# Attention and maxout FFN in one kernel: transposed attention, column halves issued alternately, one attention step per FFN step

## The chip, the cores and the metric

One core of a Trainium2 chip. The metric is device time in microseconds (us), the median over executions of the same program. Ratios are computed as the mean time of one kernel's runs over that of the other's of the same rounds, so a ratio is not quite the quotient of the medians that are quoted; intervals are 95%.

## The reference

```python
# attention with projected keys and values; B=8 batches, H=8 heads, S=1024, D=64, 64 projected rows
k_proj = einsum('ks,bhsd->bhkd', E, k)
v_proj = einsum('ks,bhsd->bhkd', F, v)
scores = q @ k_proj^T / sqrt(D)
attn   = exp(scores - max) / sum
x      = attn @ v_proj            # then heads side by side: 8192 tokens x 512
# maxout FFN
h   = max(x @ w1, x @ w2, x @ w3) # 512 -> 768
out = h @ w_out                   # 768 -> 512
```

Neither kernel subtracts the maximum before the exponential.

## The kernel before

For each batch the attention is built first and the FFN of the previous batch after it; a scheduler interleaves the two on TensorE. The matmuls of both kernels write to PSUM, a memory that is used here in pieces of 128 x 512 fp32 values, called banks. Attention has five of them, the FFN three. These parts are changed:

```python
# k projection: both halves of the heads go to partitions 0..63
for hh in range(2):
    for si in range(SI):
        matmul(out=kp_ps[0:64, hh*256:(hh+1)*256], lhsT=eT[:, si, :], rhs=k_t[:, hs, si, :])
# v projection: even heads to partitions 0..63, then odd heads to 64..127
for par, vt in ((0, vp_e), (1, vp_o)):
    for si in range(SI):
        matmul(out=vt[rows, 0:256], lhsT=fT[:, si, :], rhs=v_t[:, par::2, si, :])
...   # kpT_bd and vp_bd (block diagonals of two heads) are zeroed again for every batch
# attention times v: tokens on partitions; a column of ones in vp_bd gives the softmax sum
for si in range(8):
    for u in range(2):
        for gg in range(2):
            matmul(out=av_v[:, gg, 0:130], lhsT=pT[g][:, si, :], rhs=vp_bd[:, g, :])
        reciprocal(zinv, sums)                       # DVE
        tensor_tensor(x_sb, av, zinv, mult)          # DVE
    for ct in range(4):
        transpose(out=xt_v[:, ct, 0:128], in_=x_flat[:, ct*128:(ct+1)*128])
    copy(xT[:, :, si, :], xt_v)                      # ACT
...
# FFN, the same in both kernels: 12 matmuls of 512 columns per step, then
copy(h1s, h_ps[0])                                   # ACT
max(m12, h_ps[1], h1s); max(hT, h_ps[2], m12)        # DVE
```

The softmax here doesn't subtract the row's maximum and nothing guards it: scores larger than these inputs give would overflow.

## Time and profile before

| | before |
|---|---|
| median of 6 runs | 467.17 us (466.78 to 468.32) |
| span of the profiled execution | 465.2 us |
| TensorE busy | 93% |
| one batch (first k projection matmul to the next batch's), called the pitch below | 52.88 us |
| of it FFN, 192 matmuls x 216 ns | 41.45 us |
| last matmul starts | 459.40 us |

The profile's lines for the busy shares, the chain, one batch and the windows stand in the prediction. One more view is needed, the 40 slices of the span: a digit is the busy share of a slice in tenths (9 is 90% or more), and PEclk is the granted TensorE clock. A slice is 11.6 us. After them stand three lines of the start, DVE's timeline and TensorE's; in brackets is an idle time and who ended it.

```profile
PE   1475999999999999999999999999999999999995
PEclk9999999999999999999999999999999999999999
...
40.84 0.43 DVE L135 COPY q_p<-q_t 128x1024 bf16<-128x1024 bf16 x1 [2.51 <-DMA q_t<-in_q_dram]
41.19 0.24 DVE L209 RECIPROCAL zinv<-ps_s 128x4 f32<-128x4 f32 x2
...
41.88 0.39 PE L220 MATMUL ps_s<-ident,x_sb 128*128 128x128 bf16 x2 [2.77 <-DVE x_sb L210]
```

TensorE is full from the fifth slice on and stays full to the end. Before that, DVE waits 2.51 us for the q of the second batch, with the first batch's reciprocals behind it in its queue, and TensorE waits for them in turn. A time can therefore fall in two ways only: fewer nanoseconds of TensorE per batch, times the 7 batches that lie beside an FFN, or an earlier start. To keep the two apart, this text uses the prediction's "effective start": the start of the last matmul, less 331.8 us of FFN matmuls, less 7 times what attention and its waits hold TensorE per batch (the pitch less 41.45). For the kernel before it is 459.40 - 331.8 - 7 x 11.43 = 47.6 us. (192 x 0.216 is 41.47; 41.45 is the prediction's figure and is used throughout, which moves every effective start by the same 0.1.)

### The profile page before, as it was taken

What the parts mean: (1) busy time and instruction counts of PE and PEld (TensorE: products, weight loads), DVE (VectorE), ACT (ScalarE), POOL (GpSimd) and SP (SyncE); (2) the same over time, 40 slices, a digit from 0 to 9 for tenths busy, and PEclk for the clock granted to TensorE, in tenths of its full rate; (3) what the DMA queues carried; (4) which work ended last, traced back from release to release, by engine and by line L of the source; (5) the groups of instructions that cost most, each with busy time, mean ns of one, the idle gap of its engine ahead of it and who ended that gap; (6) DMA issues with size and microseconds to landing.
All of it is one profiled execution on the core that took longest, in us unless ns stands there. A gap on an engine that the chain in (4) does not pass through costs nothing.

```text
span 465.2 us, 6667 instructions
## 1 busy us (share of the span) xinstructions
PE 432.2 (93%) x2623; PEld 227.3 (49%) x2672; DVE 229.1 (49%) x550; ACT 173.4 (37%) x311; POOL 54.7 (12%) x74
## 2 busy tenths in 40 slices
PE   1475999999999999999999999999999999999995
PEld 1344555455544555455544555455544555444442
DVE  2026575527934375426935376425935277334351
ACT  1142555235432543235532553235432453322322
POOL 7212240004000320005000320001000000000000
PEclk9999999999999999999999999999999999999999
DMA  7999999319620691209720591202020200202102
GB/s 112 206 211 205 208 205 207 118 80 173 111 92 0 144 201 20 92 42 192 129 92 1 134 197 32 92 0 92 2 91 0 92 1 0 92 0 92 56 36 90
DMA packets 30207, 45.78 MB, mean 98 GB/s; under 512 B 1120, under 2 KB 28000, under 8 KB 28128
## 3 DMA queue, kind: packets, MB, share of 16 engines
q0 software_dynamic: 27872, 28.58, 38.1%
q1 hardware_dynamic: 2304, 16.78, 8.7%
q8 instruction: 21, 0.34, 0.3%
q14 instruction: 10, 0.08, 0.1%
HBM read 57.15 MB, written 16.78 MB: 159 GB/s over the span
## 4 chain that ended last, share of the span: by engine, by line
PE 88%; DMA 8%; issue 1%; DVE 1%; POOL 1%; ACT 0%; POOLq 0%
PE ps_m L237 53%; PE ps_m L252 18%; DMA q_t<-in_q_dram 5%; PE ps_s L220 3%; PE ps_s L154 3%; PE ps_s L200 3%; PE ps_s L108 3%; PE ps_s L141 3%; DMA k_t<-in_k_dram 2%; PE ps_s L172 2%; PE ps_s L120 0%; DVE qT_sb L147 0%; POOL q_t L101 0%; DVE x_sb L210 0%; DVE zinv L209 0%
## 5 line engine op out<-in xcount | busy, mean ns | idle before, releaser
L237 PE MATMUL ps_m<-xT,w_sb 128*128 128x512 bf16 x1109 | 263.6, 379 | 2.5 <-issue 0.7
L237 PEld LDWEIGHTS <-w_sb 128*128 128x128 bf16 x1152 | 107.6, 98 | 111.5 <-issue 3.1
L247 DVE TENSOR_TENSOR m<-ps_m,h1s 128x512 f32<-128x512 f32 x96 | 66.2, 690 | 112.5 <-PE ps_m L237 112.0
L245 ACT COPY h1s<-ps_m 128x512 f32<-128x512 f32 x96 | 56.3, 586 | 105.1 <-PE ps_m L237 104.2
L252 PE MATMUL ps_m<-wout_sb,hT 128*128 128x512 bf16 x378 | 85.1, 379 | 0.2
L248 DVE TENSOR_TENSOR hT<-ps_m,m 128x512 bf16<-128x512 f32 x96 | 66.1, 688 | 8.0 <-PE ps_m L237 1.9
L259 ACT COPY o_acc<-ps_m 128x512 f32<-128x512 f32 x64 | 37.5, 585 | 71.3 <-PE ps_m L252 68.8
L252 PEld LDWEIGHTS <-hT 128*128 128x128 bf16 x384 | 37.4, 98 | 45.1 <-DVE hT L248 3.5
L225 ACT COPY xT<-ps_s 128x512 bf16<-128x512 bf16 x58 | 34.1, 587 | 60.1 <-PE ps_s L220 60.1
L210 DVE TENSOR_TENSOR x_sb<-ps_s,zinv 128x256 bf16<-128x256 f32 x128 | 48.7, 418 | 0.2
L160 ACT ACTIVATE pT_g<-ps_s 128x512 bf16<-128x512 f32 x64 | 34.8, 596 | 20.0 <-PE ps_s L154 20.0
L220 PE MATMUL ps_s<-ident,x_sb 128*128 128x128 bf16 x256 | 35.7, 227 | 4.6 <-DVE x_sb L210 4.5
L220 PEld LDWEIGHTS <-x_sb 128*128 128x128 bf16 x256 | 22.0, 101 | 24.1 <-DVE x_sb L210 12.6
L200 PE MATMUL ps_s<-vp_bd,pT_g 128*128 128x130 bf16 x256 | 31.0, 231 | 0.5 <-DVE vp_bd L185 0.5
L101 POOL DMA_DIRECT2D k_t<-in_k_dram x16 | 11.9, 752 | 165.4 <-PE ps_s L108 161.8
L147 DVE COPY qT_sb<-ps_s 128x1024 bf16<-128x1024 bf16 x31 | 21.4, 692 | 17.5 <-PE ps_s L141 17.4
L135 POOL COPY q_p<-q_t 128x1024 bf16<-128x1024 bf16 x14 | 14.6, 1040 | 126.6 <-PE ps_s L141 110.4
L108 PE MATMUL ps_s<-k_t,eT 128*64 128x256 bf16 x128 | 17.5, 292 | 11.0 <-DMA k_t<-in_k_dram 10.7
L154 PE MATMUL ps_s<-qT_sb,kpT_bd 128*128 128x512 bf16 x64 | 20.9, 410 | 3.8 <-DVE qT_sb L147 2.4
L128 DVE COPY kpT_bd<-ps_s 64x256 bf16<-64x256 bf16 x6 | 1.7, 283 | 45.2 <-PE ps_s L120 45.2
L209 DVE RECIPROCAL zinv<-ps_s 128x4 f32<-128x4 f32 x128 | 18.0, 172 | 8.4 <-PE ps_s L200 8.1
L200 PEld LDWEIGHTS <-pT_g 128*128 128x128 bf16 x256 | 20.0, 103 | 2.8 <-DVE vp_bd L185 2.8
(39 smaller groups left out, 152.0 us busy)
## 6 DMA issues: line engine op xcount, KB each, us to landing
out_dram<-o_acc SPq DMA_DIRECT2D x16, 1024.0 KB, 3.9
q_t<-in_q_dram POOLq DMA_DIRECT2D x16, 512.0 KB, 11.4
k_t<-in_k_dram POOLq DMA_DIRECT2D x16, 512.0 KB, 8.8
v_t<-in_v_dram POOLq DMA_DIRECT2D x16, 512.0 KB, 10.9
w_sb<-in_moe_w_dram POOLq DMA_DIRECT2D x3, 768.0 KB, 22.6
wout_sb<-in_moe_w_out_dram POOLq DMA_DIRECT2D x1, 768.0 KB, 24.9
e_sb<-in_E_dram POOLq DMA_DIRECT2D x1, 128.0 KB, 3.0
f_sb<-in_F_dram POOLq DMA_DIRECT2D x1, 128.0 KB, 3.0
```

The lines of the kernel that those rows point to most:

```text
L154: nc.tensor.matmul(out=sc_ps, lhsT=kpT_bd[:, g, :], rhs=qT_sb[:, csl, :], start=True, stop=True,)
L160: nc.scalar.activation(out=pT_g[:, csl, :], in_=sc_ps, func=AF.Exp, scale=scale,)
L200: nc.tensor.matmul(out=av_v[:, gg, 0:2 * D + 2], lhsT=pT[g][:, si, :], rhs=vp_bd[:, g, :], start=(gg == 0), stop=(gg == 1),)
L210: nc.vector.tensor_tensor(out=x_sb[:, 4 * u:4 * (u + 1), :].rearrange("p (g par) d -> p g par d", par=2), in0=av_b[:, :, :, 0:D], in1=zinv ...
L220: nc.tensor.transpose(out=xt_v[:, ct, 0:P], in_=x_flat[:, ct * P:(ct + 1) * P], identity=ident,)
L225: nc.any.tensor_copy(out=xT[:, :, si, :], in_=xt_v[:, :, 0:P])
L237: nc.tensor.matmul(out=h_ps[i], lhsT=w_sb[i][:, ct, jt * P:(jt + 1) * P], rhs=rhs_x[:, ct, :, :], start=(ct == 0), stop=(ct == NCT - 1),)
L245: nc.scalar.copy(out=h1s, in_=h_ps[0])
L247: nc.vector.tensor_tensor(out=m12, in0=h_ps[1], in1=h1s, op=ALU.max)
L248: nc.vector.tensor_tensor(out=hT[:, jt, :], in0=h_ps[2], in1=m12, op=ALU.max)
L252: nc.tensor.matmul(out=o_ps, lhsT=hT[:, jt, tt * P:(tt + 1) * P], rhs=wout_sb[:, jt, :], start=(jt == 0), stop=(jt == NJT - 1),)
L259: nc.scalar.copy(out=o_acc[:, tt, :], in_=o_ps)
```

## The change

The intent: fewer small instructions around the softmax, both 64-column halves of TensorE's array busy in the projections, and an interleaving written into the program's order (Python generators: at each `yield`, one attention step for each FFN step). The core of the diff, with cuts marked:

```diff
-    ps_s = ... bufs=5   ;   ps_m = ... bufs=3
+    ps_f = ... bufs=3   ;   ps_a = ... bufs=2 (two banks each)   ;   ps_p = ... bufs=1
+    nc.scalar.preload_act_table_set("natural_log_exp_and_others")
+    ones_bd, kpT_bds[2], vp_bds[2]: zeroed and filled with ones once
+    eT2, fT2: the projection weights held twice, one copy for each column half
...
+            with tc.issue_after(ef_copy.ins if b == 0 else last_max[max(b - 2, 0)]):
+                permute()               # the copies of q before its transposes, held back
...
-        for hh in range(2):
-            for si in range(SI):
-                nc.tensor.matmul(out=kp_ps[0:KP, ...], lhsT=eT[:, si, :], ...)
+        for si in range(SI):
+            for half in range(2):
+                nc.tensor.matmul(out=kp_ps[half * HALF:(half + 1) * HALF, 0:4 * D],
+                                 lhsT=eT2[:, si, half, :], ...)
...   (the v projection likewise; the four k transposes become two)
-            for c in range(NCHUNK):     # scores and Exp, 512 columns at a time
+            pT = ...                    # one Exp of 1024 columns
+            nc.scalar.activation(out=pT, in_=sc, func=AF.Exp, scale=scale)
+            yield
+            for dst, w in ((z, ones_bd), (av, vp_bd[:, g, :])):
+                for c in range(2):
+                    nc.tensor.matmul(out=dst[:, c, :], lhsT=w, rhs=pT[:, c, :], ...)
+            nc.scalar.activation(out=zl, in_=z, func=AF.Ln)
+            nc.scalar.activation(out=zi, in_=zl, func=AF.Exp, scale=-1.0)
+            nc.vector.tensor_tensor(out=xT[:, g]..., in0=av, in1=zi, op=ALU.mult)
+            yield
-        (32 matmuls of 130 columns, 16 reciprocals, 16 multiplies, 32 transposes, 8 copies)
...
+        if b == 0:
+            spare(24)                   # matmuls on zeros, to warm the clock
...
+        for _ in main:                  # FFN of batch b, one step
+            next(side, None)            # attention of batch b+1, one step
```

## The prediction

> **What bounds the kernel now.** I read the page's busy shares first, then the chain that ended last, then TensorE's timeline for one middle batch, then the windows.
>
> ```profile
> PE 432.2 (93%) x2623; PEld 227.3 (49%) x2672; DVE 229.1 (49%) x550; ACT 173.4 (37%) x311; POOL 54.7 (12%) x74
> PE 88%; DMA 8%; issue 1%; DVE 1%; POOL 1%; ACT 0%; POOLq 0%
> ```
>
> The first line is busy time by engine, the second the chain that ended last. TensorE is both the busiest engine and nearly the whole chain; the 8% of DMA is the start. So instructions on DVE or ACT save nothing by themselves; only TensorE's stream and the first 50 us count. The timeline of TensorE (start, duration, line, operands, count) for the batch from 206.76 on:
>
> ```profile
> 206.76 1.94 PE L108 MATMUL ps_s<-k_t,eT 128*64 128x256 bf16 x16
> 208.62 1.04 PE L237 MATMUL ps_m<-xT,w_sb 128*128 128x512 bf16 x4
> ...
> 211.65 0.61 PE L141 MATMUL ps_s<-ident,q_p 128*128 128x128 bf16 x8
> 212.09 0.81 PE L237 MATMUL ps_m<-xT,w_sb 128*128 128x512 bf16 x3
> ...
> 216.70 0.60 PE L154 MATMUL ps_s<-qT_sb,kpT_bd 128*128 128x512 bf16 x2
> 217.24 1.53 PE L172 MATMUL ps_s<-v_t,fT 128*64 128x256 bf16 x16
> 218.70 0.82 PE L237 MATMUL ps_m<-xT,w_sb 128*128 128x512 bf16 x3
> ...
> 222.02 0.28 PE L220 MATMUL ps_s<-ident,x_sb 128*128 128x128 bf16 x2
> 222.13 0.40 PE L200 MATMUL ps_s<-vp_bd,pT_g 128*128 128x130 bf16 x4
> 222.37 0.27 PE L220 MATMUL ps_s<-ident,x_sb 128*128 128x128 bf16 x2
> ...
> 238.82 15.70 PE L237 MATMUL ps_m<-xT,w_sb 128*128 128x512 bf16 x70
> 254.37 5.34 PE L252 MATMUL ps_m<-wout_sb,hT 128*128 128x512 bf16 x24
> 259.64 1.61 PE L108 MATMUL ps_s<-k_t,eT 128*64 128x256 bf16 x13
> ```
>
> Cost is the distance between starts, because matmuls overlap. 72 first-layer matmuls (two records are missing) from 238.82 to 254.37 are 216 ns each. 8 q transposes take 0.44 us (55 ns each); the 16 k-projection matmuls 1.86; the 16 v-projection matmuls 1.46; 4 attention-times-v matmuls 0.24 (60 ns each). The batch takes 259.64-206.76 = 52.88 us. Its FFN is 144+48 = 192 matmuls x 0.216 = 41.45, so attention holds TensorE 11.43 us a batch. The FFN is untouched by the change.
>
> The windows (length, PE, PEld, DVE, ACT and POOL busy, clock, DMA share, GB/s) show the start:
>
> ```profile
> 0.00:50.00 50.00, 25.64 (x165) 17.01 (x167) 15.00 (x53) 13.48 (x23) 17.08 (x28) 1.00 1.11 185
> 206.80:259.70 52.90, 52.50 (x327) 27.54 (x334) 28.59 (x69) 21.03 (x38) 6.47 (x8) 1.00 0.49 100
> ```
>
> TensorE is half idle for 50 us while DMA is full, and never idle afterwards.
>
> **What the Trainium skill says.** (1) "TensorE: Matmul & The Clock Gate", Part 3, has outputs on distinct column groups running concurrently in the array. The trace agrees: read one by one, the second half of the v projection (output partitions 64 to 127) starts at 111.95 us while the first half is still starting one every 109 ns; hence 1.46 us where the k projection, all on partitions 0 to 63, needs 1.86. (2) "TensorEngine Tiling (Array Packing)", Key Properties, has a change of tiling mode drain the engine. The trace agrees: entering or leaving the 64-wide matmuls costs 93 to 96 ns, while other switches cost nothing. (3) "ScalarE: Activation LUTs", What ACT_TABLE_LOAD costs, gives 186 ns + 0.833 ns per column and an overlap of 93 ns between neighbours; here 512 columns take 597 ns and the next starts 104 ns before the end. Table sets, same page, has Exp and Ln in one set, so one load; no run here shows that yet. (4) The first page's Part 1 has a cold clock at half rate. Here 512-column matmuls are about 0.43 us apart until 48 us, though the granted clock reads 1.00.
>
> **The change part by part, per batch on TensorE.** I took the built program's order as given.
> - q transposes, 32 x 0.055 = 1.74: kept.
> - k and v projections now alternate the two column halves, 8 pairs x 0.109 = 0.87, plus two drains 0.19: 1.06 each instead of 1.86 and 1.46. Saves 1.2.
> - scores 8 x 0.216 = 1.73: kept. The k transposes become two: 0.11 instead of 0.22.
> - 32 attention-times-v matmuls and 32 x transposes (3.5 by their pitches, and their waits) become 16 matmuls of 512 columns, 8 of them a block of ones that broadcasts the softmax sum: 16 x 0.216 = 3.45. Nearly nothing.
> - Sum 1.74+2.12+1.73+0.11+3.45 = 9.15.
>
> New waits. Durations of 1024 columns from the groups: DVE tensor_tensor on PSUM is 418 ns at 256 and 690 at 512, so 1.23 us; ACT 1.03.
> - The q transposes have one PSUM bank: transposes 0.44, tail 0.26, copy 0.69 (less 0.085 overlap with its neighbour), wake-up 0.05, while only 4 FFN matmuls (0.86) stand between. About 0.09 a round: 0.3.
> - Normalisation: after the sums, Ln 1.03, Exp 1.03, multiply 1.23 in series, and the FFN's h1s copy and max stand behind them. With the next FFN step at 0: Ln starts -0.23, Exp ends 1.90, h1s ends 2.39, the multiply ends 3.2, m12 3.80, hT 4.6. Banks are wanted back at 3.02 and 3.88 when scores lie between: just met. For the last pair, the output matmuls come at once: 0.18 for the bank, 0.45 for hT, 0.63 in all.
> - Sum 10.1 instead of 11.43: 1.35 saved, times the 7 batches that lie beside an FFN: 9.4 us.
>
> DVE loses 16 reciprocal-and-multiply pairs and gains 4 long multiplies; ACT gains some 8 us of Ln and Exp over its 21; both stay below 60% of 52 us. POOL only issues.
>
> **The start.** In the old kernel the last matmul is at 459.6; 1536 FFN matmuls (331.8) and 7 x 11.43 (80.0) before it put the effective start at 47.8. In the new one, the old landings (q 13, k 18, v 23.5, third weight about 34.7 us) give k and v ready near 24.5, scores and Exp to 26.5, then four rounds of sums 0.68, Ln 1.03, Exp 1.03, multiply 1.23 and gaps: 4.15 each, as the two ACT steps and the multiply must end before the next sums get the buffer. FFN matmuls put between rounds 2 and 3 wait for the third weight and cost some 1.7. FFN proper begins near 44.9 with 9 matmuls already done: effective start 43.0, 5 us earlier, if the 24 warm-up matmuls keep the clock up; cold, about 46.5. I weigh warm 0.65: 3.8 us saved.
>
> Total: 467.2-9.4-3.8 = 454.0 us.
>
> **Rivals.**
> - The waits take back the gain. If normalisation is slower than worked out, by 0.3 us on each of Ln, Exp and multiply, every bank is late and each of four rounds costs up to 0.9 us, 3 us a batch: with 9.15+3.9 = 13 a batch the time is about 474. For it: ACT is strictly in order here and h1s always queues behind two long ops. Against it: the margins above hold with the trace's own durations. A mild form, +1 us a batch, gives 461.
> - The column halves do not overlap when alternated (the trace shows it only for streams issued one after the other): 1.75 per projection, +1.4 a batch, near 464.
> - The start stays DMA and ACT bound as before: no gain there, near 458.
> - Everything hidden: no waits, warm start: 0.93 x 7 less, 446.
>
> **Range and chances.** The sums stand on few unknowns: waits 0.3 to 2 us a batch, start 43 to 48. That gives 446 to 462. The 2% mark is 457.8; it is passed downward if waits stay below about 1.5 us a batch. Faster 0.70, within 2% 0.26, slower 0.04.
>
> **What would show it.** In the new profile: TensorE still above 90% and the chain almost all PE; a batch pitch near 51.5 us; 16 projection matmuls in about 0.9 us; idle TensorE before q transposes near 0.09 each and before the last output matmuls near 0.6; first dense FFN near 45 us with matmuls 216 ns apart. Wrong would be: a pitch of 53 with TensorE waiting for ACT h1s or DVE m12; projections at 1.75; FFN starting at 48 with matmuls at 0.43.

## The result, and the profile after

| | before | after | predicted |
|---|---|---|---|
| median, us | 467.20 (16 runs) | 451.67 (8 runs, 450.70 to 452.98) | 454.0 (446 to 462) |
| ratio | | 0.9671 [0.9659, 0.9684] | |
| batch pitch, us | 52.88 | 51.18 | 51.53 |
| saved by 7 batches, us | | 11.9 | 9.4 |
| effective start, us | 47.6 | 43.9 (43.2 in a second profile) | 44.0 (47.8 - 3.8) |

The two savings, 7 x 1.70 = 11.9 and 47.6 - 43.9 = 3.7, add up to 15.6. By the definition of the effective start that is how much earlier the last matmul starts (459.40 against 443.83); the medians differ by 15.5.

The page of the kernel after has these busy times, these slices and this chain that ended last:

```profile
PE 424.0 (94%) x2253; PEld 201.4 (45%) x2296; DVE 212.4 (47%) x323; ACT 193.1 (43%) x273; POOL 26.0 (6%) x36
...
PE   6675999999999999999999999999999999999994
PEclk9759899999999999999999999999999999999999
...
PE 87%; DMA 6%; ACT 2%; issue 2%; DVE 1%; POOL 1%; POOLq 0%; DVEq 0%
```

ACT is busier by 20 us, DVE less by 17 with 227 fewer instructions, and neither matters: the chain is still nearly all TensorE. The PEclk row shows something new, a granted clock of 7 and 5 tenths in the second and third slices.

The window of the first 50 us (length, busy time of PE, PEld, DVE, ACT and POOL, clock, DMA share, GB/s) answers to that of before:

```profile
0.00:50.00 50.00, 32.55 (x160) 15.02 (x163) 16.45 (x33) 15.48 (x17) 13.78 (x22) 0.80 1.12 187
```

TensorE is busy for 32.55 us of it instead of 25.64, but 8.11 of these are the warm-up matmuls, which compute nothing, and the clock averages 0.80. The window of a middle batch (206.20 to 257.40) has TensorE busy for 50.78 of 51.20 us, as full as before; the batch is shorter because there is less in it.

TensorE's timeline of the middle batch (start, duration, line, operands, count; in brackets an idle time and who ended it):

```profile
206.22 1.06 PE L151 MATMUL ps_p<-k_t,eT 128*64 128x256 bf16 x16
207.21 1.68 PE L231 MATMUL ps_f<-xT,w_sb 128*128 128x512 bf16 x7
...
211.53 1.06 PE L178 MATMUL ps_p<-v_t,fT 128*64 128x256 bf16 x16
212.53 2.76 PE L231 MATMUL ps_f<-xT,w_sb 128*128 128x512 bf16 x11
...
243.62 1.79 PE L249 MATMUL ps_f<-wout_sb,hT 128*128 128x512 bf16 x7
245.61 3.63 PE L249 MATMUL ps_f<-wout_sb,hT 128*128 128x512 bf16 x16 [0.21 <-DVE hT L242]
249.08 2.75 PE L231 MATMUL ps_f<-xT,w_sb 128*128 128x512 bf16 x12
...
255.04 1.03 PE L231 MATMUL ps_f<-xT,w_sb 128*128 128x512 bf16 x4
255.99 0.61 PE L138 MATMUL ps_p<-ident,q_p 128*128 128x128 bf16 x8
```

Start to start, each projection takes 1.00 us (207.21 - 206.22 and 212.53 - 211.53). The 24 output matmuls from 243.62 take 5.46 instead of 24 x 0.216 = 5.18: they wait 0.27. Before the q transposes at 255.99, four FFN matmuls take 0.95 instead of 0.86: a wait of 0.08. (Some rows count 23 or 11 where the program has 24 or 12; those records are missing, the distances are not.) All engines around the last normalisation of that batch, ACT and DVE rows:

```profile
240.79 1.02 ACT L214 ACTIVATE zl<-ps_a 128x1024 f32<-128x1024 f32 x1 [1.52 <-PE ps_a L210]
241.85 1.06 ACT L216 ACTIVATE zi<-zl 128x1024 f32<-128x1024 f32 x1
242.81 0.57 ACT L239 COPY h1s<-ps_f 128x512 f32<-128x512 f32 x1
242.94 1.22 DVE L217 TENSOR_TENSOR xT<-ps_a,zi 128x1024 bf16<-128x1024 f32 x1 [1.88 <-PE ps_f L231]
...
244.86 0.69 DVE L242 TENSOR_TENSOR hT<-ps_f,m 128x512 bf16<-128x512 f32 x1
```

The series Ln, Exp, multiply is there, and behind it the FFN's own copy and maxima: hT ends at 245.55 and the output matmuls that need it go on at 245.61.

The start, TensorE's timeline again:

```profile
26.98 1.01 PE L210 MATMUL ps_a<-pT,ones_bd 128*128 128x512 bf16 x2 [1.11 <-ACT pT L204]
31.23 1.01 PE L210 MATMUL ps_a<-pT,ones_bd 128*128 128x512 bf16 x2 [1.11 <-ACT pT L204]
34.58 0.57 PE L231 MATMUL ps_f<-xT,w_sb 128*128 128x512 bf16 x1 [0.64 <-DMA w_sb<-in_moe_w_dram]
36.70 0.59 PE L210 MATMUL ps_a<-pT,ones_bd 128*128 128x512 bf16 x2 [1.11 <-ACT pT L204]
40.40 0.59 PE L210 MATMUL ps_a<-pT,ones_bd 128*128 128x512 bf16 x2 [1.41 <-ACT pT L204]
...
45.50 3.64 PE L231 MATMUL ps_f<-xT,w_sb 128*128 128x512 bf16 x9 [0.24 <-ACT h1s L239]
```

The rounds of sums start 4.25, 5.47 and 3.70 us apart: cold, cold with a wait for the third weight (34.58), warm. Two 512-column matmuls that read 1.01 instead of 0.59 are cold: the clock is low, and such matmuls start 0.43 us apart instead of 0.216. At 45.50 nine FFN matmuls take 3.48 to the next start (48.98) instead of 1.94, so they are cold again.

### The profile page after: what moved, and what is told of

The parts are those of the page before. It is cut to its first block, busy times and chain, and to the rows that moved or that the text cites. A ratio compares the mean times of both kernels' runs of the same rounds, so it can differ in the third digit from the quotient of the medians.

```text
span 450.0 us, 5616 instructions
## 1 busy us (share of the span) xinstructions
PE 424.0 (94%) x2253; PEld 201.4 (45%) x2296; DVE 212.4 (47%) x323; ACT 193.1 (43%) x273; POOL 26.0 (6%) x36
## 4 chain that ended last, share of the span: by engine, by line
PE 87%; DMA 6%; ACT 2%; issue 2%; DVE 1%; POOL 1%; POOLq 0%; DVEq 0%
PE ps_f L231 55%; PE ps_f L249 18%; DMA w_sb<-in_moe_w_dram 6%; PE ps_a L210 5%; PE ps_p L138 3%; PE ps_a L197 3%; PE ps_p L178 2%; PE ps_p L151 2%; ACT zi L216 0%; DVE hT L242 0%; DVE m L241 0%; ACT zl L214 0%; ACT pT L204 0%; POOL w_sb L100 0%; DVE xT L217 0%
## 5 line engine op out<-in xcount | busy, mean ns | idle before, releaser
L231 PE MATMUL ps_f<-xT,w_sb 128*128 128x512 bf16 x1122 | 265.5, 381 | 4.9 <-DVE xT L217 2.4
L241 DVE TENSOR_TENSOR m<-ps_f,h1s 128x512 f32<-128x512 f32 x96 | 66.2, 689 | 120.4 <-PE ps_f L231 118.8
L239 ACT COPY h1s<-ps_f 128x512 f32<-128x512 f32 x96 | 55.7, 581 | 89.0 <-PE ps_f L231 74.3
L249 PE MATMUL ps_f<-wout_sb,hT 128*128 128x512 bf16 x378 | 86.7, 379 | 0.8 <-DVE hT L242 0.6
L217 DVE TENSOR_TENSOR xT<-ps_a,zi 128x1024 bf16<-128x1024 f32 x32 | 39.2, 1225 | 69.2 <-PE ps_f L231 39.5
L242 DVE TENSOR_TENSOR hT<-ps_f,m 128x512 bf16<-128x512 f32 x96 | 66.4, 692 | 9.2
L256 ACT COPY o_acc<-ps_f 128x512 f32<-128x512 f32 x64 | 37.3, 583 | 51.1 <-PE ps_f L249 50.7
L214 ACT ACTIVATE zl<-ps_a 128x1024 f32<-128x1024 f32 x32 | 32.7, 1023 | 45.8 <-PE ps_a L210 41.4
L204 ACT ACTIVATE pT<-ps_a 128x1024 bf16<-128x1024 f32 x32 | 32.8, 1024 | 24.4 <-PE ps_a L197 24.4
L216 ACT ACTIVATE zi<-zl 128x1024 f32<-128x1024 f32 x32 | 33.8, 1056 | 1.0
```

The costliest lines, as they stand in the source:

```text
L204: nc.scalar.activation(out=pT, in_=sc, func=AF.Exp, scale=scale)
L216: nc.scalar.activation(out=zi, in_=zl, func=AF.Exp, scale=-1.0)
L217: nc.vector.tensor_tensor(out=xT[:, g].rearrange("a (c si) p -> a c (si p)", c=2), in0=av, in1=zi, op=ALU.mult,)
L231: nc.tensor.matmul(out=h_ps[i], lhsT=w_sb[i][:, ct, jt * P:(jt + 1) * P], rhs=rhs_x[:, ct, :, :], start=(ct == 0), stop=(ct == NCT - 1),)
L239: nc.scalar.copy(out=h1s, in_=h_ps[0])
L241: nc.vector.tensor_tensor(out=m12, in0=h_ps[1], in1=h1s, op=ALU.max)
```

## The experiments

My theory after the result: per batch the gain is TensorE time saved by the projections, less waits that are smaller than predicted; the start gains despite a cold clock, and what is left there is clock and weights. The rivals: the gain is really that of the new normalisation, or of the warm-up; the alternation of the halves is worth nothing; ACT is nearly the bound; the remaining waits are tied to where a step stands in the order.

Twelve kernels ran, in three groups that each shared a chip and the runs of the kernel before. All gave a correct result.

| run | us | ratio to before | pitch, us |
|---|---|---|---|
| after, again | 451.95 | 0.9667 [0.9647, 0.9687] | 51.18 |
| no warm-up | 452.19 | 0.9670 [0.9647, 0.9693] | 51.18 |
| kept warm | 447.50 | 0.9569 [0.9550, 0.9588] | 51.18 |
| normalisation one step earlier | 454.29 | 0.9723 [0.9700, 0.9746] | 51.51 |
| halves in turn | 458.34 | 0.9813 [0.9789, 0.9836] | 52.10 |
| before, v halves alternating | 463.83 | 0.9938 [0.9916, 0.9959] | 52.42 |
| second Ln | 455.16 | 0.9744 [0.9718, 0.9770] | 51.13 |
| old normalisation | 450.31 | 0.9634 [0.9611, 0.9657] | 51.39 |
| normalisation one step later | 449.69 | 0.9623 [0.9608, 0.9637] | 50.89 |
| first FFN group held | 449.93 | 0.9631 [0.9613, 0.9648] | 51.17 |
| warm and later | 445.39 | 0.9544 [0.9523, 0.9564] | 50.89 |
| warm, later, old first | 442.69 | 0.9477 [0.9463, 0.9492] | 50.89 |

### The yardstick: the changed kernel again

No edit.

> The changed kernel itself once more, as the yardstick on this chip. Both theories: ratio to before near 0.967, batch pitch 51.18 us, about 451.7 us.

451.95 us, pitch 51.18, effective start 43.2. The batch repeats to a hundredth of a microsecond; the start does not. In this execution TensorE was warm from 27.9 to 37, cold to 40 and warm after, where the first profile had it cold to about 35. The clock in the first 50 us is a matter of the execution, so starts must be compared by the medians of several runs, and single profiles of starts differ by a microsecond or so.

### Halves in turn: the alternation undone

```diff
-        for si in range(SI):
-            for half in range(2):
+        for half in range(2):
+            for si in range(SI):
```
and the same for the v projection.

> In the changed kernel the two column halves of both projections run one after the other instead of alternating. If alternation is where the projections gain: 16 matmuls take 1.46 us as the v projection of before did, not 1.00, twice a batch: pitch 52.1, 7 x 0.92 = 6.4 us longer, about 458. Rival: what was gained there came from elsewhere (fewer waits, other placing): within 1 us of 451.7.

Pitch 52.10, 0.92 more than after. TensorE's timeline of this run:

```profile
209.41 1.53 PE L151 MATMUL ps_p<-k_t,eT 128*64 128x256 bf16 x16
210.87 1.68 PE L231 MATMUL ps_f<-xT,w_sb 128*128 128x512 bf16 x7
```

210.87 - 209.41 = 1.46 instead of 1.00. The same 16 matmuls, the same operands, only the order differs. The alternation is worth 6.4 us of the whole (7 x 0.92), and the times of the two groups differ by as much, 458.34 - 451.95 = 6.4; of the pieces tested it is the largest.

### The kernel before with its v projection alternating

```diff
-        for par, vt in ((0, vp_e), (1, vp_o)):
-            for si in range(SI):
+        for si in range(SI):
+            for par, vt in ((0, vp_e), (1, vp_o)):
...   (the line that sets rows moves with them)
```

> The kernel before, with the v projection alone alternating its halves: the one part of the change that needs nothing else. 16 matmuls in 1.00 us instead of 1.46, pitch 52.42 instead of 52.88, 7 x 0.46 = 3.2 us shorter, ratio 0.993. Rival: in that frame a wait takes its place (the DVE and ACT copies behind it are no earlier): ratio 1.000.

Pitch 52.42 instead of 52.88, time 463.83 against 466.83. The projection takes 1.00 in the old kernel too:

```profile
215.83 1.06 PE L172 MATMUL ps_s<-v_t,fT 128*64 128x256 bf16 x16
216.83 0.82 PE L237 MATMUL ps_m<-xT,w_sb 128*128 128x512 bf16 x3
```

So the effect belongs to the order of the matmuls and to nothing else in the new kernel: two lines exchanged in the old one bring a fifth of the whole gain.

### The old normalisation in the new kernel

```diff
-  (z and av matmuls, Ln, Exp, one multiply into xT)
+  (8 x: 4 matmuls of 130 columns, reciprocal, multiply, 4 transposes, ACT copy)
```
The vp_bd tiles get their columns of ones back; the FFN, the projections and the generators stay.

> The changed kernel with the old normalisation and x transposes (32 matmuls of 130 columns, 32 transposes, DVE reciprocal and multiply) put back. By pitches TensorE needs 3.5 us against 3.45, so I expect the batch pitch within 0.4 us of 51.18. At the start the first FFN needs only the first half of the rounds: it could begin near 38 us rather than 44.4, up to 4 us shorter: 447 to 452. Rival: the new normalisation is a main part of the gain: pitch above 51.8 and 456 or more.

450.31 us: not slower than the changed kernel, if anything faster. The pitch is 51.39 (51.74 once), so the new normalisation saves 0.2 us a batch; but the effective start is 40.95 instead of 43.2 to 43.9. With one batch alone on the chip, the old way has many short steps on TensorE, DVE and ACT that overlap, while the new one has four long rounds. The old way also finishes tokens block by block: in this run's trace the FFN starts at 36.20, with half of the blocks done, where the new one can finish no FFN group before its fourth multiply (44.45). The most conspicuous part of the change gives about 1.5 us to the seven batches and takes some 2 to 3 from the start.

### No warm-up

```diff
-        if b == 0:
-            spare(24)
```

> The 24 warm-up matmuls are left out. My reading of the trace: they hold the clock up only until about 17.8 us, and what sets the start is the third weight landing at 34.6 us and the four normalising rounds after it; q transposes become about 0.5 us slower three times, which the wait for the weight mostly absorbs: 0 to 0.7 us longer, 452. Rival: the warm-up is what bought the 3.9 us of the start: 3 us or more longer, 455.

452.19 us, not to be told from 451.95. In the profile everything up to the first sums is 0.93 later (27.91 instead of 26.98), and the first dense FFN begins 0.7 later. That is not shown to be the warm-up's doing: the second profile of the unchanged kernel has its first sums at 27.93 too, with the warm-up in. That the 24 warm-up matmuls make the start (the rival, 455) falls: they are worth less than the noise between such runs, some 1.5 us.

### Kept warm

```diff
+            if b == 0:
+                spare(4)      # after each qT copy; likewise 3 or 4 after kp_sb, kpT_bd and
+                              # each Exp, and 4 or 8 after each multiply
```
The spare matmuls write a bank that nobody reads and stand where TensorE would idle.

> More idle matmuls fill the waits of the first attention up to the first FFN. If the cold clock costs there: rounds near 4.2 us, and the first 21 FFN matmuls at 216 ns, so the first q transposes of the second batch start near 47.8 us instead of 48.98: 1.2 us shorter, about 450.5. Rival: the chain of Exp, Ln, Exp and multiply alone sets the start: no change, or some tenths longer, as 9 FFN matmuls are no longer done early. Pitch 51.18 in both.

447.50 us, 4.4 less than the yardstick. I had expected about 1.2, so the size was missed by far. Granted clock by slice, then TensorE's timeline, of this run:

```profile
PEclk9999999999999999999999999999999999999998
```

```profile
33.85 0.59 PE L218 MATMUL ps_a<-pT,ones_bd 128*128 128x512 bf16 x2
...
37.55 0.59 PE L218 MATMUL ps_a<-pT,ones_bd 128*128 128x512 bf16 x2
...
38.41 2.11 PE L241 MATMUL ps_f<-xT,w_sb 128*128 128x512 bf16 x9
```

Every round is 3.70 (37.55 - 33.85) and warm. Two things differ from the changed kernel: the clock never falls, and the scheduler put the first FFN matmuls after the last round (38.41), so that no round waits for the third weight. The traces also say where the time went. The first q transposes of the second batch start at 44.59 instead of 48.98, 4.39 earlier: 0.54 before the first sums, 2.31 in the three distances between rounds (11.11 instead of 13.42), 1.54 in the nine FFN matmuls that were cold. Of the 2.31, the wait for the weight is 1.22 (5.47 against the 4.25 of a cold round without it); the remaining 3.2 of the 4.4 stand where the clock differs. The next run takes them apart by experiment.

### First FFN group held, no spare matmuls

```diff
+                        if b == 0 and ch == 0 and jt == 0:
+                            with tc.issue_after(last_av[0]):
+                                mm()
```

> Tells apart the two things that keeping warm changed: no idle matmuls are added, but the first FFN matmuls are held behind the last attention matmul, so the third weight holds nothing up. If the weight was most of those 4.4 us: the start shortens by 3 to 4 us, 448. If the clock was most: rounds of 4.25 us without the 1.2 us wait, 0.7 to 1.2 us shorter, about 451, with matmuls still 0.43 us apart in the record.

449.93 us, 1.7 to 2.0 less than the changed kernel (by ratio and by medians of different groups). TensorE's timeline:

```profile
35.42 1.01 PE L210 MATMUL ps_a<-pT,ones_bd 128*128 128x512 bf16 x2 [1.11 <-ACT pT L204]
...
39.67 1.01 PE L210 MATMUL ps_a<-pT,ones_bd 128*128 128x512 bf16 x2 [1.11 <-ACT pT L204]
...
41.33 4.24 PE L232 MATMUL ps_f<-xT,w_sb 128*128 128x512 bf16 x12
```

The wait for the weight is gone and all rounds are 4.25 apart, cold. The held group then starts cold as well, but being dense it brings the clock back by 45.8. From here to the kept-warm run, 2.4 us remain, and that run has the same order of FFN work and a warm clock. So both count, and the time lies between the two that I had expected (448 if the weight was most of it, 451 if the clock was). The split is not exact: holding the group also changes when the clock recovers, and in this run the nine FFN matmuls after it are warm.

### Normalisation one step earlier, and one step later

Earlier takes away the `yield` after the kpT_bd copies; later adds one after the v projection. Nothing is computed differently, but every score and sum stands beside another FFN step.

```diff
 # earlier                         # later
-        yield                     +        yield
```

> One pause between side steps is removed, so the last normalisation of a batch comes one FFN step earlier and is no longer the step before the last output matmuls. If their waits there are what the trace shows (0.37 for hT and 0.12 for the bank): pitch 50.7 instead of 51.18, 7 x 0.49 = 3.4 us shorter, about 448.3. Rival: the waits come back at another bank or step: pitch 51.1 to 51.3, no change.

> One more pause between side steps, the opposite shift: the last normalisation now stands between the last FFN step and the output matmuls, so hT is made before its multiply. If the trace's 0.27 us a batch before the outputs (0.15 and 0.12) is the multiply standing ahead of m12 and hT: pitch 50.91 instead of 51.18, 7 x 0.27 = 1.9 us shorter, about 450. Rival: the wait moves, as in the earlier shift: pitch 51.2 or more.

Earlier: pitch 51.51, worse by 0.33, where I had expected 50.7. From 243.62 on in the changed kernel the output matmuls wait 0.27; with the step moved that wait went, but the same wait came back before the first chunk's outputs (5.46 for 24 matmuls from 219.94 in this run), and a new one before an FFN bank, since after the last normalisation two FFN steps follow with no scores between them:

```profile
239.21 3.62 PE L230 MATMUL ps_f<-xT,w_sb 128*128 128x512 bf16 x16
243.00 1.89 PE L230 MATMUL ps_f<-xT,w_sb 128*128 128x512 bf16 x8 [0.17 <-DVE m L240]
244.72 5.34 PE L248 MATMUL ps_f<-wout_sb,hT 128*128 128x512 bf16 x23
```

24 matmuls take 244.72 - 239.21 = 5.51 instead of 5.18: that is the 0.33. My theory ("the wait disappears when the step moves") fell. The rival ("the waits come back elsewhere") held in kind, but its figure (51.1 to 51.3) was too low, as a second wait came on top.

Later: pitch 50.89, as expected (50.91), and 449.69 us. Now the step after the last sums is the output stage itself, whose hT was ready:

```profile
244.12 5.34 PE L250 MATMUL ps_f<-wout_sb,hT 128*128 128x512 bf16 x24
249.30 2.75 PE L232 MATMUL ps_f<-xT,w_sb 128*128 128x512 bf16 x12
```

5.18 for 24 matmuls, no wait. The 0.27 was thus a matter of where the last normalisation stands.

### A second Ln: is ACT nearly the bound?

```diff
             nc.scalar.activation(out=zl, in_=z, func=AF.Ln)
+            nc.scalar.activation(out=zl, in_=z, func=AF.Ln)
```

> Each Ln is done twice, 1.02 us more on ACT per normalisation. If the bank margins of my prediction are right: the second bank comes 0.57 us late at two of the steps and the outputs wait 0.95 us longer, 2.1 us a batch, pitch 53.3; with some 3 us more at the start about 469. Rival: ACT has slack, at 43% busy: pitch near 51.2 and only the start longer, 454 to 456.

This puts 4 x 1.02 us more on ACT per batch, in the middle of the series that the prediction's margins hang on. I had expected a pitch of 53.3; it was 51.13, no longer than before the edit. The time grew to 455.16 through the start alone (effective start 48.2). Its rounds of sums are 5.30, 5.18 and 4.76 apart in this run's trace instead of 4.25, 5.47 and 3.70: two are a microsecond longer, and in the middle one the wait for the weight is hidden. ACT and DVE around the last normalisation:

```profile
246.91 0.58 ACT L240 COPY h1s<-ps_f 128x512 f32<-128x512 f32 x1
247.37 1.07 ACT L217 ACTIVATE zi<-zl 128x1024 f32<-128x1024 f32 x1
247.52 0.69 DVE L242 TENSOR_TENSOR m<-ps_f,h1s 128x512 f32<-128x512 f32 x1 [2.33 <-ACT h1s L240]
```

The scheduler did not leave the order alone: h1s now stands before the second Exp, and the maximum before the multiply, so the FFN queues behind neither. The run shows that ACT has the slack for 4 us more per batch. It does not test the margins of the unchanged order, which stay untested: I found no edit that lengthened the series and surely kept the order.

### Warm and later, and the best version

The first puts the kept-warm and one-step-later edits together. The second also uses the old normalisation for the first batch only, where nothing hides the long rounds, and lets the attention of batch 1 begin one FFN step later (in place of that batch's additional step):

```diff
+        if b == 0:  (old normalisation, with spare matmuls between its parts)
+        else:       (new normalisation)
...
+        for step, _ in enumerate(main):
+            if b > 0 or step > 0:
+                next(side, None)
```

> Kept warm and the last normalisation later together. If the two are independent (one is the start, one the batches): 447.5 - 1.9 = 445.6. Rival: they overlap and 447.5 stays.

> As the one before, with the old normalisation for the first batch alone, whose first half is enough to start the FFN, and the second batch's attention one FFN step later. Put back for all batches it began the FFN at 36.2 us and saved 3 us of start while cold; kept warm I expect the first dense FFN near 37 us and 1 to 3 us less than the combination without it: 442.5 to 444.5. Rival: the start is then bound by the loads (weights until 38 us, q of the second batch until 43 us): no gain, 445.6.

445.39 (expected 445.6): the two gains add, so neither takes anything from the other. 442.69 for the last (expected 442.5 to 444.5), with an effective start of 37.4 and the first FFN matmul at 35.86. It beats both kernels: 0.9477 of the time before.

## Why the prediction was right, point by point

- **What bounds the kernel.** Right: TensorE 94%, chain 87% TensorE; 8 us of additional Ln and Exp per batch on ACT cost nothing by themselves. ACT's sum grew by less than the prediction's 8, from 21.03 to 23.89 us in a middle batch, because the copies of xT, 34 us in all on ACT, fell away; the prediction left that out. That Ln and Exp need one load of tables came true: the trace has one ACT_TABLE_LOAD, of 1.28 us.
- **The projections.** Right, and tested from both sides. Predicted 1.06 each with two drains; measured 1.00 from their first matmul to the next start plus 0.09 on entering. Nearly half of the old k projection's excess came from using one half of the array only (1.86 to 1.46), the rest from the order (1.46 to 1.00).
- **Scores, k transposes, sums and attention times v.** Right: scores 1.73, transposes 0.11, sums and attention times v 3.45. "Nearly nothing" is 0.2 in the old-normalisation run. The prediction's own pitches give as much: 32 x 0.060 + 32 x 0.055 is 3.7 and not its 3.5, against 3.45. Its "other switches cost nothing" is not quite so either: the old k transposes (64 rows) start 0.31 us after the FFN matmul before them instead of 0.216, and that cost is gone as well.
- **The waits.** The mechanism was right, the size too large. The terms "About 0.09 a round: 0.3" and "0.63 in all" measured 0.18 (0.08, 0.08 and 0.02) and 0.27, together 0.45 instead of 0.93. Banks that were "just met" were met: no wait there. That is the mis-sized term, by 0.48; q transposes and drains measured 0.1 more than predicted, which leaves 0.35 in the pitch (51.53 - 51.18), and 7 x 0.35 = 2.4 us is the difference between 454.0 and 451.7. The durations used were right (Ln 1.02, Exp 1.06, multiply 1.22 in the lines above).
- **Adding up.** k 1.00, v 1.00, entering 0.19, k transposes 0.11, q transposes 1.79, scores 1.73, sums and av 3.45, waits 0.45: 9.72 a batch, against 51.18 - 41.45 = 9.73 measured. Of the 1.70 saved per batch, runs show 0.92 for the order of the halves, 0.40 for the k projection's second half (1.86 to 1.46) and 0.21 for the normalisation; the 0.17 left is about what the k transposes save (0.11 by the prediction, and 0.09 for the switch), which no run takes alone.
- **The start.** The number was right (3.8 predicted; 3.7 and 4.4 in two profiles), its reasons only in part, so this half of the agreement is partly luck. The 3.8 itself is a slip: 0.65 x 4.8 + 0.35 x 1.3 is 3.6 (and the last matmul of the kernel before is at 459.4, not 459.6). "4.15 each, as the two ACT steps and the multiply must end before the next sums get the buffer" names the wrong last step: in the profile the second sums start at 31.23, before the first multiply ends at 31.41, and the idle time is ended by the Exp of the scores. The round is Ln, Exp, the next Exp of scores and the sums, 3.70 warm and 4.25 cold; that it is about as long as the 4.15 predicted is chance. "If the 24 warm-up matmuls keep the clock up" did not come true: the clock fell again from about 18 us. The wait for the third weight was there at 34.58 (34.7 predicted) and cost 1.2, not 1.7. And the start's gain is not from the normalisation, which costs time there, but from what stands before it; which of the other parts (order of loads and transposes, projections, block diagonals made once) brings how much was not taken apart. Two of them stand out in the traces. The new kernel transposes q at 13.61, before k is projected, where the old one did it at 21.00 and after; its first sums start at 26.98, the old attention times v at 35.45. And the 2.51 us that DVE waits for the second batch's q in the kernel before are gone, as the new kernel holds these copies back (they start at 46.89). Neither the prediction nor the theory above named that wait, and no run tests it alone.
- **The rivals.** Waits that take back the gain: fell, for this order. Halves that do not overlap: fell. No gain at the start: fell.

## What to carry to other kernels

If a matmul uses only 64 columns of the array, send neighbouring matmuls to alternating halves: exchanging two loops was worth more here than rewriting the softmax. When a side task is placed between steps of a main task, try each place: one step earlier and one later were 0.33 us worse and 0.29 better per batch, with nothing computed differently. In this kernel the stage that stands alone wanted short overlapping steps and a TensorE that is never half idle, and the stage that hides behind another wanted few TensorE cycles; the best version used one form for the first batch and another for the rest.

## What the Trainium skill lacked or had wrong

- "TensorE: Matmul & The Clock Gate", Part 1, names idle windows of about 3.4 us as what makes the clock fall, and the section on the second failure mode says that frequent small idle times make it oscillate. What happened looks like the second: no idle time between 12 and 45 us exceeded 2.4 us, yet matmuls were cold from about 18 to 35 us in one execution, and from about 17 to 27 and 37 to 40 in another. The page gives no busy share that is enough; filling the idle times (from the second slice on, TensorE 80% busy or more) kept it warm, and the kept-warm version took 4.4 us less, 1.2 of them by an order without the wait for a weight.
- "TensorE: Matmul & The Clock Gate", Part 1, warns that recorded clock events have been seen to be unreliable. It does not say that the reported clock can read full through a whole cold start: in the kernel before, it read 9 in all slices while 512-column matmuls were 0.43 us apart until 48 us. The kernel without warm-up reported 0.995, and with warm-up 0.975, at the same speed.
- "TensorE: Matmul & The Clock Gate", Back-to-back issue gap, gives 131 ns for sustained 512-column matmuls with their weight loads and 81 ns for 128 columns. Here they were 216 and 55 ns, which is what that section calls the isolated gap.
- The same page, Part 3, has no number for the order of issue on two column halves. Here 16 matmuls of 256 columns took 1.87 us on one half, 1.46 on two halves in turn and 1.00 alternating.
- "TensorEngine Tiling (Array Packing)", Key Properties, names the drain on a change of mode but no size: 0.09 us on entering the 64-wide matmuls, and as much on leaving them.
